# Written order of every engine's instructions for the whole program, instead of for its first part only: delta rule and gated feed-forward on one core

## The chip, the cores and the metric

The kernel runs on one core of a Trainium2 chip. The time is the device time of one execution in microseconds: before the change 883.39 us, the median of three runs (882.07 to 884.29). The profiled execution has a span of 881.3 us.

A core has a matrix engine (PE, TensorE), VectorE (DVE in the profile), ScalarE (ACT), GpSimd (POOL) and SyncE (SP), which here only issues DMAs. Each of them works through its own stream of instructions in the order of the stream, and waits for the others through semaphores. The question of this case is only the order of the streams.

## The reference

Two blocks follow one another. The first is the delta rule over 768 tokens, for 4 batches of 8 heads with 48 elements each:

```python
k_n = k / (np.linalg.norm(k, axis=-1, keepdims=True) + 1e-06)
for t in range(S):
    y[:, :, t] = einsum('bhd,bhde->bhe', q[:, :, t], state)
    v_old = einsum('bhde,bhd->bhe', state, kt)
    state = state + bt * einsum('bhd,bhe->bhde', kt, vt - v_old)
```

The second is a gated feed-forward on the result, seen as 3072 tokens of 384 elements, with 1536 inner columns:

```python
xn = x / sqrt(mean(x * x) + 1e-06) * rms_g
g = xn @ w_gate
out = (g * sigmoid(g) * (xn @ w_val)) @ w_out
```

All is in float32. The weights arrive as 64-bit numbers, and the kernel itself turns them into float32.

## The kernel before

The 768 tokens of a sequence are cut into 6 chunks of 128. A chunk of one batch is a unit, so a chunk has 4 units and the program 24. Inside a chunk the recurrence is solved in blocks: the scores of keys against keys give a triangular matrix for each head, whose 32-wide diagonal blocks are inverted on VectorE for all batches and heads at once. This is `invert`: 31 pairs of a product `tmp` and a sum into `ttb`. The inverse goes to DRAM as `td`, and a second matrix as `nd`; from there `tt` and `ne` are read back in the layout that PE needs.

```python
def invert(c, dt):
    nc.gpsimd.memset(ttb, 0.0)
    ...
    for i in range(W - 1):                       # W = 32
        nc.vector.scalar_tensor_tensor(out=tmp, in0=gblk[...], scalar=nbeta[...], in1=ttb[...], ...)
        nc.vector.tensor_tensor(out=to, in0=to, in1=tmp, op=ALU.add)     # to: part of ttb
        ...
        yield dt
    nc.sync.dma_start(out=td, in_=ttb)
    nc.vector.tensor_tensor(out=gblk, in0=ttb..., in1=nbeta..., op=ALU.mult)
    for b in range(B):
        for a in (1, 3, 0, 2):
            nc.sync.dma_start(out=tt[b][...], in_=td[...])
        if b == 0:
            nc.sync.dma_start(out=nd, in_=gblk)
        for a in (0, 2):
            nc.sync.dma_start(out=ne[...], in_=nd[...])
    yield dt
```

`gblk`, the scores that `invert` starts from, comes the same way through DRAM: `gather` sends the blocks `gd` on ScalarE's queue, unit by unit, and after the fourth unit `gblk` is read on SP's queue. Ahead of that stands `prepare`, for each unit: the norm of the keys (a square on ScalarE, a sum on VectorE, a power on GpSimd), transposes of queries and keys on PE (`p_t`), scores (`p_g`), their copies on ScalarE and masked copies on VectorE.

`recur` is the chain of a chunk. Its steps `corner` (small products `p_v` and `p_w`, which read `tt` and `ne`), `inner` (`p_z`, `p_x`) and `outer` (`p_k`, `p_y`, `p_s`) are run for four units, shifted against one another:

```python
for s in range(-3, B + 2):
    inner(s, s - 1, s + 1)
    yield dt
    outer(s + 1, s - 1)
    yield dt
    corner(s + 3, s + 2)
    ... # scale and transpose the results of units s - 1 and s - 2 (p_xt)
    yield dt
```

`ffn` is the feed-forward of two units, 256 tokens. It has 12 steps f; the output product `leave` of a step comes one step later, so that the silu on ScalarE and the product `h_f` on VectorE have time:

```python
def ffn(m, f0, f1):
    ...
    for f in range(f0, f1):
        p_gv = psum.tile([128, 2, TOK], FP32, name="p_gv", tag="gv", bufs=2)
        for i, w_sb in enumerate((wg_sb, wv_sb)):
            for t in range(KT):                                   # KT = 3
                nc.tensor.matmul(p_gv[:, i], w_sb[:, t, ...], xt[:, t], ...)
            yield 1
        nc.scalar.activation(out=sil, in_=p_gv[:, 0], func=ACTF.Silu)
        nc.vector.tensor_tensor(out=h_f, in0=sil, in1=p_gv[:, 1], op=ALU.mult)
        if last is not None:
            leave(f - 1, last)                                    # two matmuls, 128x384: p_o
            yield 1
        last = h_f
    yield 0.9
    leave(f1 - 1, last)
    ...
```

At the end of an `ffn` two outputs thus stand next to each other. The first two feed-forwards (m = 0 and 1) are run in halves of 6 steps, because the weights are still being converted on VectorE (`weights`: five instructions of 128x768 for each block of weights, written with their own times).

All these parts are Python generators. A plan gives each a start time, and the number that a generator yields is the time to its next piece. The plan is run in order of time, in its own units, about one for three gate matmuls; what it writes is the program:

```python
def at(time, gen):
    plan.append((time, len(plan), gen))

def run_plan(until=math.inf):
    heap = plan
    heapq.heapify(heap)
    while heap and heap[0][0] < until:
        t, i, gen = heapq.heappop(heap)
        dt = next(gen, None)
        if dt is not None:
            heapq.heappush(heap, (t + dt, i, gen))

TF = 68
CYC = 3 * FT * B // 2                                             # 72
at(0, setup())
...
at(49, recur(0, 1.5, 3))
for i, m in enumerate((0, 1, 0, 1)):
    at(TF + CYC // 4 * i, ffn(m, half_f * (i // 2), half_f * (i // 2 + 1)))
...
for c in range(1, NCH):
    t0 = TF - 16 + CYC * c
    first = TF + 2 if c == 1 else t0 - 60
    for b in range(B):
        at(first + 4.5 * b, prepare(B * c + b))
    at(first + 27, invert(c, 0.68))
    at(*((t0 - 4, recur(c, 0.9)) if c == 1 else (t0 - 9, recur(c, 1.2))))
    for g in range(B // 2):
        at(t0 + 16 + CYC // 2 * g, ffn(B // 2 * c + g, 0, FT))
with tc.manual_schedule():
    run_plan(TF + CYC // 2)
run_plan()
```

What is written inside `tc.manual_schedule()` stays, on each engine, in the order in which it is written. What is written outside of it is put in order by the framework's scheduler, which goes by its own estimates of when each instruction can run; it may also set such instructions between those of the first group.

Of the kernel before, what the change touches and what calls it, by code (L numbers as in the profile page):

```python
# [27 lines left out]
def kernel(  # L28
# [739 lines left out]
    plan = []  # L768
# [1 line left out]
    def at(time, gen):  # L770
        plan.append((time, len(plan), gen))

    def run_plan(until=math.inf):
        heap = plan
        heapq.heapify(heap)
        while heap and heap[0][0] < until:
            t, i, gen = heapq.heappop(heap)
            dt = next(gen, None)
            if dt is not None:
                heapq.heappush(heap, (t + dt, i, gen))  # L780


    TF = 68
    CYC = 3 * FT * B // 2
# [25 lines left out]
        for g in range(B // 2):  # L810
            at(t0 + 16 + CYC // 2 * g, ffn(B // 2 * c + g, 0, FT))
    with tc.manual_schedule():
        run_plan(TF + CYC // 2)
    run_plan()


# [28 lines left out]
```

## Time and profile before

| | |
|---|---|
| time | 883.39 us (882.07 to 884.29) |
| span of the profiled execution | 881.3 us |
| PE busy | 828.5 us, 94% |
| weight loads of PE (PEld) busy | 646.7 us, 73% |
| VectorE busy | 404.7 us, 46% |
| ScalarE busy | 259.0 us, 29% |
| GpSimd busy | 97.7 us, 11% |
| gate and value products (p_gv) in the chain that ended last | 36% of the span |
| output products (p_o) in that chain | 18% |
| tmp and ttb of the inversion in that chain | 4% and 3% |
| mean granted clock of PE | 0.96 |

The page divides the span into 40 slices of 22 us and gives for each the busy tenths of every engine and the clock that PE was granted, in tenths of full speed. In the timeline a line has start and length in us, engine, source line, operation, output and inputs, shapes and the number of instructions merged; in brackets stands how long the engine was idle ahead of it and what released it. PE's matmuls are pipelined, so that the lengths of neighbours overlap; what the matmuls take is read from start to start.

### The profile page before, as it was taken

What the parts mean: (1) busy time and instruction counts of PE and PEld (TensorE: products, weight loads), DVE (VectorE), ACT (ScalarE), POOL (GpSimd) and SP (SyncE); (2) the same over time, 40 slices, a digit from 0 to 9 for tenths busy, and PEclk for the clock granted to TensorE, in tenths of its full rate; (3) what the DMA queues carried; (4) which work ended last, traced back from release to release, by engine and by line L of the source; (5) the groups of instructions that cost most, each with busy time, mean ns of one, the idle gap of its engine ahead of it and who ended that gap; (6) DMA issues with size and microseconds to landing.
All of it is one profiled execution on the core that took longest, in us unless ns stands there. A gap on an engine that the chain in (4) does not pass through costs nothing.

```text
span 881.3 us, 19880 instructions
## 1 busy us (share of the span) xinstructions
PE 828.5 (94%) x8434; PEld 646.7 (73%) x8434; DVE 404.7 (46%) x997; ACT 259.0 (29%) x691; POOL 97.7 (11%) x136
## 2 busy tenths in 40 slices
PE   6487798989999999999999999999999999999998
PEld 5376665767877777787777787777787777777776
DVE  3786677886243393243392243492332491221110
ACT  4622345511424312324311324212334212221101
POOL 3000144200041000131000131000130000010000
PEclk8576799999999999999999999999999999999999
DMA  7615536502222103122103122103121103000000
GB/s 182 169 45 133 145 98 157 151 2 75 57 56 49 46 18 86 31 63 39 47 18 85 38 56 41 46 18 85 39 55 23 36 23 80 2 20 1 18 1 18
DMA packets 150935, 51.81 MB, mean 59 GB/s; under 512 B 142368, under 2 KB 145440, under 8 KB 150848
## 3 DMA queue, kind: packets, MB, share of 16 engines
q1 hardware_dynamic: 124736, 47.40, 21.2%
q10 hardware_dynamic: 26112, 3.15, 2.2%
q8 instruction: 66, 1.08, 0.5%
q14 instruction: 21, 0.17, 0.1%
HBM read 36.37 MB, written 14.16 MB: 57 GB/s over the span
## 4 chain that ended last, share of the span: by engine, by line
PE 72%; DVE 9%; DMA 2%; ACT 2%; issue 1%; POOL 1%; ACTq 0%; SPq 0%
PE p_gv L732 36%; PE p_o L719 18%; DVE tmp L428 4%; DVE ttb L437 3%; PE p_g L329 3%; PE p_y L531 2%; PE p_t L313 2%; PE p_k L569 2%; PE p_z L587 2%; PE p_y L569 2%; PE p_x L605 1%; PE p_v L497 1%; PE p_z L596 1%; DMA gblk<-gd 1%; PE p_s L550 1%; DVE h_f L743 1%
## 5 line engine op out<-in xcount | busy, mean ns | idle before, releaser
L719 PE MATMUL p_o<-wo_sb,h_f 128*128 128x384 f32 x576 | 215.8, 497 | 11.1 <-DVE h_f L743 11.1
L732 PE MATMUL p_gv<-xt,wg_sb 128*128 128x256 f32 x864 | 217.3, 388 | 0.0
L732 PE MATMUL p_gv<-xt,wv_sb 128*128 128x256 f32 x864 | 213.6, 383 | 0.0
L732 PEld LDWEIGHTS p_gv<-xt,wg_sb 128*128 128x128 f32 x864 | 161.6, 193 | 39.4 <-issue 0.6
L732 PEld LDWEIGHTS p_gv<-xt,wv_sb 128*128 128x128 f32 x864 | 161.5, 190 | 24.4 <-issue 2.5
L743 DVE TENSOR_TENSOR h_f<-sil,p_gv 128x256 f32<-128x256 f32 x144 | 60.1, 418 | 241.3 <-ACT sil L741 241.1
L741 ACT ACTIVATE sil<-p_gv 128x256 f32<-128x256 f32 x144 | 55.1, 383 | 342.8 <-PE p_gv L732 314.7
L719 PEld LDWEIGHTS p_o<-wo_sb,h_f 128*128 128x128 f32 x576 | 104.0, 190 | 62.7 <-DVE h_f L743 16.7
L428 DVE SCALAR_TENSOR_TENSOR tmp<-gblk,nbeta,ttb 128x31 f32<-128x31 f32 (+15 forms) x186 | 74.7, 402 | 11.5 <-DMA gblk<-gd 4.7
L437 DVE TENSOR_TENSOR ttb<-ttb,tmp 128x31 f32<-128x31 f32 (+15 forms) x186 | 63.6, 342 | 6.6 <-PE p_g L329 0.5
L343 DVE TENSOR_TENSOR gp<-p_g,mask 64x128 f32<-64x128 f32 (+1 forms) x160 | 37.9, 277 | 40.0 <-ACT gp L339 35.6
L329 PE MATMUL p_g<-kqt 64*64 64x192 f32 (+2 forms) x896 | 46.3, 331 | 9.5 <-ACT gp L339 4.8
L329 PEld LDWEIGHTS p_g<-kqt 64*64 64x64 f32 x896 | 34.1, 147 | 20.1 <-ACT gp L339 6.5
L293 POOL TENSOR_TENSOR knrm<-ksum,half 128x8 f32<-128x8 f32 x24 | 42.4, 1765 | 2.0
L688 POOL TENSOR_SCALAR ms<-ms 128x1 f32<-128x1 f32 x24 | 5.9, 247 | 328.0 <-ACT y L680 327.8
L318 ACT COPY kqt<-p_t 128x512 f32<-128x512 f32 x48 | 28.0, 584 | 40.2 <-PE p_t L313 37.9
L420 POOL MEMSET ttb<- 128x1024 f32 x6 | 6.1, 1021 | 261.5 <-DMA td<-ttb 246.0
L587 PEld LDWEIGHTS p_z<-v_raw,tt 64*64 64x64 f32 x768 | 26.1, 142 | 8.8 <-issue 6.7
L512 ACT COPY vs<-p_v 32x256 f32<-32x256 f32 x48 | 17.4, 362 | 49.4 <-PE p_w L504 28.1
L338 ACT COPY gp<-p_g 128x128 f32<-128x128 f32 x96 | 25.5, 265 | 20.3 <-PE p_g L329 18.4
L605 PE MATMUL p_x<-tt,gp 64*64 64x64 f32 x384 | 29.0, 229 | 1.8 <-ACT tt L514 1.8
L531 PE MATMUL p_y<-u,gp 128*64 128x48 f32 x768 | 26.6, 222 | 3.4 <-DVE u L612 3.2
(87 smaller groups left out, 798.6 us busy)
## 6 DMA issues: line engine op xcount, KB each, us to landing
kpad<-in_k_dram SPq DMA_DIRECT2D x24, 192.0 KB, 2.6
raw<-in_moe_w_gate_dram SPq DMA_DIRECT2D x6, 768.0 KB, 5.0
qpad<-in_q_dram SPq DMA_DIRECT2D x24, 192.0 KB, 2.8
raw<-in_moe_w_val_dram SPq DMA_DIRECT2D x6, 768.0 KB, 4.7
v_raw<-in_v_dram SPq DMA_DIRECT2D x24, 192.0 KB, 3.0
raw<-in_moe_w_out_dram SPq DMA_DIRECT2D x6, 768.0 KB, 4.3
out_dram<-o_sb SPq DMA_DIRECT2D x24, 192.0 KB, 1.9
gd<-gp ACTq DMA_DIRECT2D x96, 32.0 KB, 1.7
```

The costliest lines, as they stand in the source:

```text
L293: nc.gpsimd.tensor_tensor(out=knrm, in0=ksum, in1=half, op=ALU.pow)
L329: nc.tensor.matmul(to, pair[d, K1 if i else K0], pair[d, places], skip_group_check=True)
L343: nc.vector.tensor_tensor(out=to[p, :, place], in0=p_g[p, :, place], in1=mask[p, i, None].to_broadcast([p.stop, 2, HC]), op=ALU.mult,)
L428: nc.vector.scalar_tensor_tensor(out=tmp, in0=gblk[:, i, None, i + 1 :].to_broadcast(shape), scalar=nbeta[:, c, i : i + 1], in1=ttb[:, 0 : ...
L437: nc.vector.tensor_tensor(out=to, in0=to, in1=tmp, op=ALU.add)
L531: nc.tensor.matmul(p_y[p, h], gp[b_y][:, h, HC * place : HC * (place + 1)], u[:, h], start=(c == 0 and h == 0), stop=True, skip_group_chec ...
L587: nc.tensor.matmul(p_zs[b_z][p, h], tt[b_z][p, h], r[p, h], start=(h == 0), stop=(p is lo), skip_group_check=True,)
L605: nc.tensor.matmul(p_x[lo, h], gp[b_x][hi, h, HC * K0 : HC * (K0 + 1)], tt[b_x][hi, h], skip_group_check=True,)
L719: nc.tensor.matmul(p_o[i], h_f[:, i * C : (i + 1) * C], wo_sb[:, f], start=(f == f0), stop=(f == f1 - 1),)
L732: nc.tensor.matmul(p_gv[:, i], w_sb[:, t, f * 128 : (f + 1) * 128], xt[:, t], start=(t == 0), stop=(t == KT - 1),)
L741: nc.scalar.activation(out=sil, in_=p_gv[:, 0], func=ACTF.Silu)
L743: nc.vector.tensor_tensor(out=h_f, in0=sil, in1=p_gv[:, 1], op=ALU.mult)
```

## The change

The plan is no longer run in two parts. The whole of it is written inside `tc.manual_schedule()`, so that each engine follows the plan's order to the end, where before the scheduler ordered everything with a plan time of 104 (TF + CYC/2) or later. It is meant to give the author of the plan, not the scheduler's estimates, the last word on what each engine does next. No instruction is added, removed or altered.

```diff
-    def run_plan(until=math.inf):
-        heap = plan
+    def run_plan():
+        heap = list(plan)
         heapq.heapify(heap)
-        while heap and heap[0][0] < until:
+        while heap:
             t, i, gen = heapq.heappop(heap)
             dt = next(gen, None)
             if dt is not None:
@@
     with tc.manual_schedule():
-        run_plan(TF + CYC // 2)
-    run_plan()
+        run_plan()
```

## The prediction

> **What bounds the kernel now.** I read the page first, then the granted clock and busy times by stage, then who PE waits for, then PE's and VectorE's instructions in order of time around each wait. The page's busy slices:
>
> ```profile
> PE   6487798989999999999999999999999999999998
> DVE  3786677886243393243392243492332491221110
> PEclk8576799999999999999999999999999999999999
> ```
>
> A slice is 22 us. From the tenth on PE is full; before that it has holes and a low clock. A busy PE row proves little, since ends of matmuls are modelled, so I timed the work. Each matmul leaves two records. In the timeline one feed-forward step f (six gate and value matmuls, two output matmuls) takes 2.59 + 1.29 = 3.88 us wherever nothing else lies between, and that is the same at 198 us and at 870 us. There are 144 such steps: 144 x 3.88 = 559 us. A chunk of the recurrence repeats every 130.5 us (its double output product is at 451.3, 581.8 and 712.3); 24 steps are 93 us of it and the remaining 37 are PE's recurrence matmuls. So PE bounds the kernel, and only PE's own idle time can be won or lost. Who PE waited for after 200 us:
>
> ```profile
> PE p_o L719 <- DVE h_f L743: 4.1, 5, 1.6
> ```
>
> The columns are total, times, longest. Only 4 us are idle in the last 680, so the change can win almost nothing there. The rest of the idle time lies before 200 us. Where the regions of old and new order meet, PE shows:
>
> ```profile
> 179.55 1.56 PE L719 MATMUL p_o<-wo_sb,h_f 128*128 128x384 f32 x4 [1.08 <-DVE h_f L743]
> 180.94 1.46 PE L732 MATMUL p_gv<-xt,wg_sb 128*128 128x256 f32 x6
> 182.24 1.46 PE L732 MATMUL p_gv<-xt,wv_sb 128*128 128x256 f32 x6
> 186.41 1.60 PE L719 MATMUL p_o<-wo_sb,h_f 128*128 128x384 f32 x4 [2.72 <-DVE h_f L743]
> 187.81 2.76 PE L732 MATMUL p_gv<-xt,wg_sb 128*128 128x256 f32 x6
> 190.37 1.88 PE L732 MATMUL p_gv<-xt,wv_sb 128*128 128x256 f32 x6
> ```
>
> Counting steps from 1, these are output 11, gates 13, output 12, gates 14. Output 12 waits for VectorE's product h_f of step 12, which stands behind weight conversion and the inversion of chunk 1:
>
> ```profile
> 185.08 0.95 DVE L274 SCALAR_TENSOR_TENSOR wo_sb<-raw,wo_sb 128x768 f32<-128x768 uint32 x1
> 185.95 0.41 DVE L743 TENSOR_TENSOR h_f<-sil,p_gv 128x256 f32<-128x256 f32 x1
> ```
>
> VectorE runs there without a gap, so it, not PE, sets the pace until 187. And gates 14, 4.3 us instead of 2.6, are slow: the granted clock is 0.50 from 188 to 190 and 0.70 to 192, a penalty of 1.7 us after the wait.
>
> **What the Trainium skill says.** "TensorE: Matmul & The Clock Gate", section "Part 1: The HAM clock gate", has the clock halved after an idle window of about 3.4 us, with a free-running window. The trace agrees in kind: 2.7 us idle at 184 and 3.1 at 147 are each followed by a clock near 0.5; 1.6 us idle at 450 is not. The same page's "Architectural detail" section says that ScalarE's and VectorE's queues are strict FIFO. The trace agrees: every wait above is a product queued behind other work. "Perfetto Trace Analysis", section "Identifying the Most-Contended Engine", calls matmul busy time a bad measure of headroom; here 98% busy and the timed steps happen to agree.
>
> **The change part by part.** No instruction is added or removed. What was in written order only for plan times below 104 is now so throughout. Placing the streams of both builds side by side:
>
> (1) PE. Identical up to output 11, and again from about step 25 on, save single outputs and the choice of buffers. Between, output 12 moves ahead of gates 13, and the first recurrence product of chunk 1 (p_v) comes after output 17 instead of after gates 20. The chain itself is more spread between steps.
>
> Working for chunk 1. VectorE's stream is the same to the product of step 12, so output 12 still starts at 186.4, but gates 13 now lie after it instead of inside the wait: PE idles from 180.9 to 186.4, 5.5 us, and is 2.6 behind. From 187.8: gates 13 to 18 are 6 x 2.59 = 15.5, outputs 13 to 17 are 5 x 1.29 = 6.5, the slow clock 1.7 again; PE is at p_v at 211.5. Does the inverse arrive? Now td (the inverse, to DRAM) is issued at:
>
> ```profile
> 210.41 0.34 SPq L445 DMA_DIRECT2D td<-ttb  x1
> ```
>
> In the new order VectorE doesn't wait 1.33 us for a gate product at 192.7 and has one product fewer (0.33) ahead of it, and its later products come after their gates; hence about 209.2 (some 0.5 open). The new order sends the first tt blocks ahead of nd, as the first chunk does in both kernels; there p_v ran 5.3 us after td (62.5 to 67.8). So p_v starts at 214.5, with PE idle 3.0. At 218.4 the kernel before had done p_v, gates 19 and 20, outputs 18 and 19. The new one needs after 214.5: 0.6 for p_v and 2 x 3.88, and is there at 222.9: **4.5 us behind**, plus 0.9 for an even chance of another 1.7 us slow clock.
>
> What comes back: before, the rest of that chain is dense. From 218.4 to the last transpose of chunk 1 (269.4) are 51.0 us with six steps (23.3) and two key or query transposes (0.9): 26.8 for the chain. In the chunk starting at 471.0, whose steps alternate as the new order has them, the same stretch is 66.6 minus ten steps (38.8), minus transposes and scores (2.8), minus p_v (0.6): 24.4. The dense one runs v and w, z and x one after the other, where the spread one mixes them on different rows (0.69 for v and w together, 0.62 each alone). So **-2.5 us**. Chunk 1: 4.5 + 0.9 - 2.5 = +2.9.
>
> (2) VectorE in the inversions of chunks 2 to 5. PE's order is the same there, but the products h_f sit elsewhere between the 31 pairs of tmp and ttb. At the end of a feed-forward of 12 steps two outputs stand back to back, and the second waits for its h_f. Before, in the chunk at 581:
>
> ```profile
> 581.01 0.42 DVE L437 TENSOR_TENSOR ttb<-ttb,tmp 128x255 f32<-128x255 f32 x1
> 581.36 0.41 DVE L743 TENSOR_TENSOR h_f<-sil,p_gv 128x256 f32<-128x256 f32 x1
> ```
> ```profile
> 581.82 1.56 PE L719 MATMUL p_o<-wo_sb,h_f 128*128 128x384 f32 x4 [0.74 <-DVE h_f L743]
> ```
>
> 14.5 pairs and two products precede that h_f; in the new order 16 pairs and three do. Extra: 1.5 pairs x 0.95 + 0.33 = 1.75. But the new inversion may start ahead of a product it now stands behind: gblk is issued at 564.74, lands 3.3 later (page, median), and the sends on ScalarE come about 0.35 later behind one silu, so 568.4 instead of 568.95: -0.55. Net **+1.2 us each, four times: +4.8**. In the chunk at 451 the wait is 1.6 already and 2.8 might drop the clock; I leave this to the range.
>
> (3) ScalarE, GpSimd and SP. Key norms of the next chunk come later, silu stands behind copies and ksq. I followed each silu and h_f through one chunk with the durations before (silu 0.38, eight gp copies 2.2, four sends 1.8, ksq 0.5, the power on GpSimd 1.67): the latest are 0.5 to 2 us ahead of their outputs, so nothing on PE's path. The closest is the output at 520.0, with 0.5 us left. Nothing in (3) is counted.
>
> Sum: 883.4 + 2.9 + 4.8 = **891**.
>
> **Rivals.** First: the written order is the better tuned one, and the time falls. For it: its chain in chunk 1 is denser in mixed products, and hoisted norms no longer hold up VectorE (it waited 1.8 us for one at 157). Against it: VectorE then waits for gblk at 176.9 anyway, and PE's idle time after 200 us is 4 us in all. At best the first wait costs nothing and the h_f shift vanishes: 881. Second: a strict order turns small delays into stalls in each chunk, for instance tt blocks of the second batch behind nd and ne, or silu behind ksq, at 0.5 us margins. With two such stalls of 1 us per chunk and slow clocks behind each wait: 900 to 905. Third: all of it hides, since PE's order hardly differs: 884 to 886; against that stand outputs 12 and p_v, which are pinned by VectorE.
>
> **Range and chances.** Chunk 1 may be +1 to +6, by tt's landing and the clock; chunks 2 to 5 +2 to +9. Together 886 to 897 holds eight in ten. 2% is 17.7 us: 866 can't be reached with 4 us of idle time to win; 901 needs the second rival in every chunk.
>
> **What would show it.** PE idle about 5.5 us ahead of the output at 186.4; p_v idle 2 to 4 us near 212, released by tt; about 1 to 2 us more wait for h_f at each double output (near 321, 453, 584, 714); other PE waits absent. Wrong would be: td well below 209, gblk landing earlier, so that h_f comes in time, or waits on ScalarE in the recurrence.

## The result and the profile after

The changed kernel takes **889.15 us** (median; 887.27 to 890.23) against 883.07 us (882.07 to 884.29) for the kernel before, measured side by side: a ratio of 1.0066, with a 95% interval of 1.0044 to 1.0088. It is 6 us slower, 0.7%. Its profiled execution has a span of 886.8 us. Its page has these busy slices:

```profile
PE   5487798968999999999999999999999999999998
DVE  3786577995234293233393234392233491221010
PEclk9577699988999999999999999999999999999999
```

From the eleventh slice on PE is as full as before. Apart from small differences in the first five slices, where both kernels have the same order on PE, the ninth and tenth differ, some 177 to 222 us: PE has 6 and 8 tenths where it had 8 and 9, and the clock 8 and 8 where it had 9 and 9. Who PE waited for from 170 us to the end (line, releaser; total, times, longest):

```profile
PE p_o L719 <- DVE h_f L743: 11.4, 6, 5.3
PE p_v L497 <- DMA tt<-td: 2.7, 4, 1.7
```

The second group didn't exist before. PE's timeline of the changed kernel in the two places where the prediction put the loss, output 12 and the first recurrence product of chunk 1:

```profile
178.78 1.56 PE L719 MATMUL p_o<-wo_sb,h_f 128*128 128x384 f32 x4 [1.37 <-DVE h_f L743]
185.65 2.93 PE L719 MATMUL p_o<-wo_sb,h_f 128*128 128x384 f32 x4 [5.31 <-DVE h_f L743]
...
209.59 1.45 PE L719 MATMUL p_o<-wo_sb,h_f 128*128 128x384 f32 x4
212.78 0.22 PE L497 MATMUL p_v<-tt,gp 32*32 32x32 f32 x2 [1.74 <-DMA tt<-td]
213.51 1.05 PE L497 MATMUL p_v<-tt,gp 32*32 32x32 f32 x30 [0.51 <-DMA tt<-td]
214.49 2.93 PE L719 MATMUL p_o<-wo_sb,h_f 128*128 128x384 f32 x4
217.22 2.77 PE L732 MATMUL p_gv<-xt,wg_sb 128*128 128x256 f32 x6
219.78 1.65 PE L732 MATMUL p_gv<-xt,wv_sb 128*128 128x256 f32 x6
221.26 1.46 PE L732 MATMUL p_gv<-xt,wg_sb 128*128 128x256 f32 x6
```

The wait of output 12 is 5.31 us instead of 2.72, and p_v waits 1.74 and 0.51 us for tt, where PE didn't wait before. What follows p_v is slow, too: from start to start output 18 takes 2.73 us instead of 1.29, and the two halves of gates 19 take 2.56 and 1.48 instead of 1.29 each. That is 1.44 + 1.27 + 0.19 = 2.9 us lost. The stretch from 214 us by granted clock (columns: stretch, length, busy time and instructions of PE, PEld, DVE, ACT and POOL, clock, DMA share, GB/s):

```profile
214.00:220.00 6.00, 6.00 (x31) 4.19 (x28) 1.11 (x2) 0.73 (x2) 0.00 (x0) 0.50 0.43 115
```

At the double outputs of the later chunks the changed kernel waits 1.33, 1.17, 1.09 and 1.09 us for h_f, where the kernel before waited 0.75, 1.61, 0.74 and 0.74. The wait that corresponds to the one shown of the kernel before at 581.82, in PE's timeline and then in VectorE's:

```profile
586.98 1.56 PE L719 MATMUL p_o<-wo_sb,h_f 128*128 128x384 f32 x4 [1.09 <-DVE h_f L743]
```
```profile
586.51 0.41 DVE L743 TENSOR_TENSOR h_f<-sil,p_gv 128x256 f32<-128x256 f32 x1
```

And one thing that the prediction had named only in a rival. In chunk 2 SP's queue issues nothing for 4.5 us after `nd`:

```profile
341.15 0.39 SPq L461 DMA_DIRECT2D nd<-gblk  x1
345.67 0.80 SPq L463 DMA_DIRECT2D ne<-nd  x2
346.51 1.92 SPq L456 DMA_DIRECT2D tt<-td  x4
```

`ne` can't be read before `nd` has landed, and the tt blocks of the second batch stand behind it. p_v of that batch runs about 1.0 us after PE reached it, in two waits (348.54 and 349.16).

**Where the 6 us came from.** The order up to output 11 is the same in both kernels, and its start differs by chance (179.55 before, 178.78 after), so I count from there. From output 11 to the first double output: 140.36 us before, 145.17 after, that is +4.81, of which 0.58 is that output's own longer wait. Then from double output to double output +0.77, +0.35 and +0.35, and from the last to the end 168.96 against 168.95. So in these two profiles chunk 1 costs 4.2 us and all later ones 2.1, together 6.3.

### The profile page after: what moved, and what is told of

The parts are those of the page before. It is cut to its first block, busy times and chain, and to the rows that moved or that the text cites. A ratio compares the mean times of both kernels' runs of the same rounds, so it can differ in the third digit from the quotient of the medians.

```text
span 886.8 us, 19834 instructions
## 1 busy us (share of the span) xinstructions
PE 827.0 (93%) x8434; PEld 644.8 (73%) x8434; DVE 404.6 (46%) x997; ACT 256.0 (29%) x691; POOL 96.4 (11%) x136
## 4 chain that ended last, share of the span: by engine, by line
PE 67%; DVE 11%; DMA 5%; ACT 2%; issue 1%; SPq 0%; ACTq 0%; POOL 0%; DVEq 0%
PE p_gv L732 33%; PE p_o L719 16%; DVE tmp L428 5%; DVE ttb L437 4%; PE p_g L329 3%; PE p_y L531 2%; DMA gblk<-gd 2%; PE p_t L313 2%; PE p_k L569 2%; PE p_z L587 2%; PE p_y L569 2%; DMA gd<-gp 1%; PE p_x L605 1%; PE p_v L497 1%; DVE h_f L743 1%
## 5 line engine op out<-in xcount | busy, mean ns | idle before, releaser
L719 PE MATMUL p_o<-wo_sb,h_f 128*128 128x384 f32 x576 | 217.0, 500 | 14.5 <-DVE h_f L743 14.5
L680 ACT ACTIVATE y<-p_y 128x384 f32<-128x384 f32 x24 | 11.8, 491 | 92.6 <-PE p_y L531 92.6
```

The source lines that it names most:

```text
L719: nc.tensor.matmul(p_o[i], h_f[:, i * C : (i + 1) * C], wo_sb[:, f], start=(f == f0), stop=(f == f1 - 1),)
```

## The experiments

The theory was that of the prediction: VectorE pins output 12 and p_v in chunk 1, and h_f is late at the double outputs of the later chunks. The times below were measured beside the kernel before (883.2 us or within 0.4 of it each time). A single execution of the kernel before came out anywhere from 878.5 to 886.4 us, and the intervals show that a ratio is good to 1 to 2 us. The last column of the table removes part of that scatter from the profiled execution: it is the span less the start of output 11. In ten of these executions, the kernel before among them, whose PE order is the same up to output 11, that start lay anywhere from 178.0 to 181.9 us. The column still stands for one execution each, and not always a usual one: the profiled execution was the fastest of its kernel with the scheduler from 104 to 176 only (884.85 against a median of 888.21), with the last outputs later (885.67 against 889.35) and with the chain later and nd first (881.59 against 884.12), and the slowest with nd first (890.58 against 888.66).

| kernel | median, us | ratio to before (95%) | output 11 to the end, us |
|---|---|---|---|
| before | 883.07 | 1 | 701.8 |
| changed | 889.15 | 1.0066 (1.0044 to 1.0088) | 708.0 |
| written order up to plan time 176 | 885.65 | 1.0041 (1.0022 to 1.0061) | 703.6 |
| scheduler from 104 to 176 only | 888.21 | 1.0063 (1.0040 to 1.0085) | 704.8 |
| output 12 later | 888.40 | 1.0071 (1.0049 to 1.0093) | 706.5 |
| chain of chunk 1 later | 884.84 | 1.0020 (1.0007 to 1.0033) | 702.6 |
| last outputs later | 889.35 | 1.0066 (1.0045 to 1.0087) | 708.7 |
| nd first | 888.66 | 1.0052 (1.0036 to 1.0069) | 706.6 |
| useless products in both waits | 887.09 | 1.0040 (1.0026 to 1.0054) | 705.0 |
| chain later, last outputs later, nd first | 881.04 | 0.9975 (0.9959 to 0.9991) | 700.9 |
| chain later, last outputs later | 884.26 | 1.0016 (1.0001 to 1.0032) | 703.5 |
| chain later, nd first | 884.12 | 1.0013 (1.0003 to 1.0024) | 701.2 |
| chain later, useless products at output 12 | 882.52 | 0.9996 (0.9984 to 1.0009) | 700.1 |
| the three and useless products | 884.54 | 1.0025 (1.0012 to 1.0037) | 703.9 |

### Half of the change at a time

The plan is cut at 176 (TF + CYC*3/2), which separates chunk 1 from the rest, save that the preparation and the inversion of chunk 2, planned from 136 and 163 on, begin before the cut. The two edits are shown against the kernel before.

```diff
 # written order up to plan time 176
     with tc.manual_schedule():
-        run_plan(TF + CYC // 2)
+        run_plan(TF + CYC * 3 // 2)
     run_plan()
```

> The written order holds up to plan time 176 (TF + CYC*3/2), the scheduler's from there on, so that chunk 1 has the changed kernel's order and chunks 2 to 5 that of the kernel before. Theory (most of the loss is in chunk 1: output 12 pinned ahead of gates 13, p_v ahead of its data, slow clock after both): about 887.5, 4 to 5 us above the kernel before. Rival (most of the loss is the shifted h_f and the late tt in chunks 2 to 5, as my prediction's sum had it with 4.8 of 7.7): about 885 to 886.

```diff
 # scheduler from 104 to 176 only
     with tc.manual_schedule():
         run_plan(TF + CYC // 2)
-    run_plan()
+    run_plan(TF + CYC * 3 // 2)
+    with tc.manual_schedule():
+        run_plan()
```

> The complement: the scheduler orders what has plan times from 104 to 176 (chunk 1), everything else is in written order. PE's stream is then that of the kernel before throughout, and VectorE's, ScalarE's and SP's are the changed kernel's from chunk 2 on. Theory: about 885, 2 us above the kernel before (0.35 to 0.6 more wait at each of three double outputs, 1 us for late tt in chunk 2). Rival: 887 to 888. The two costs should add up to the 6 us of the whole change within 1 us.

The first half costs 3.6 us by its ratio (0.0041 x 883), the second 5.6; the profiles, counted from output 11, give 1.8 and 3.0. My expectations of the sizes fell: both medians lie where the rivals had them (885.65 and 888.21), and the two costs don't add up to 6 within 1 us. Each half shows the waits that were expected of it: the first has 5.31 us at output 12 and 1.84 and 0.41 at p_v, and the usual 0.73 at the later double outputs; the second has the old 2.72 at output 12 and, from chunk 3 on, 1.25, 1.16 and 1.22 at the double outputs. So both parts of the prediction exist. Their sizes aren't settled by this pair: the medians add up to 9.2, the profiles to 4.8, and the whole is 6. The profile of the second half is that of its fastest execution. In the first half the scheduler moved an output between the gates in chunk 2, so that its first double output doesn't wait at all, which may make it cheaper than chunk 1 of the whole change; this isn't shown.

### Is VectorE what pins chunk 1?

If output 12 waits because it stands too early on PE, a later place wins 2.6 us. If VectorE sets the pace anyway, p_v waits longer instead.

```diff
 # output 12 later: after gates 13, as before
-        p_o = [psum.tile([128, DM], FP32, name="p_o", tag="out", bufs=2) for i in range(2)]
+        p_o = []                                  # the two tiles are taken at the first leave
 ...
-        yield 0.9
+        yield 2.9 if (m, f0) == (1, 0) else 0.9
```

The output tiles `p_o` are taken later here, and likewise in each edit below that moves the last outputs.

> The changed kernel, with only the last output of the second feed-forward half two plan units later, behind gates 13 as in the kernel before. Theory (VectorE, not PE, sets when p_v can start, so what PE saves at output 12 it waits at p_v): the wait at output 12 falls from 5.3 to about 2.7 us, the one at p_v grows from about 2.4 to about 5, and the time stays at 888 to 889. Rival (the two waits are independent costs): 2.6 us or more are won, 886.

Nothing is won: 1.0071 against 1.0066. Output 11 and PE's waits behind it in its timeline:

```profile
180.32 1.56 PE L721 MATMUL p_o<-wo_sb,h_f 128*128 128x384 f32 x4 [1.28 <-DVE h_f L745]
187.19 1.56 PE L721 MATMUL p_o<-wo_sb,h_f 128*128 128x384 f32 x4 [2.72 <-DVE h_f L745]
193.73 1.56 PE L721 MATMUL p_o<-wo_sb,h_f 128*128 128x384 f32 x4 [2.39 <-DVE h_f L745]
214.10 0.28 PE L497 MATMUL p_v<-tt,gp 32*32 32x32 f32 x2 [3.29 <-DMA tt<-td]
```

The wait is down to 2.72 as in the kernel before, but 2.39 us reappear at the next output and p_v waits 3.29 + 0.29 instead of 1.74 + 0.51. Counted from the start of output 11, p_v's first products start at 33.78 us here and at 34.00 in the changed kernel (214.10 - 180.32 and 212.78 - 178.78), although PE's waits ahead of them differ; with all last outputs later and with useless products, both below, it is 33.82 and 33.64. So PE doesn't set this time: the inverse must be finished on VectorE and have been through DRAM.

The counter-test lets PE do feed-forward work while it would wait for tt: the chain of chunk 1 starts three plan units later.

```diff
 # chain of chunk 1 later
-        at(*((t0 - 4, recur(c, 0.9)) if c == 1 else (t0 - 9, recur(c, 1.2))))
+        at(*((t0 - 1, recur(c, 0.8)) if c == 1 else (t0 - 9, recur(c, 1.2))))
```

> The changed kernel, with the chain of chunk 1 started 3 plan units later and run at 0.8 instead of 0.9 per piece; p_v then stands behind gates 20. Theory: the wait for tt (2.4 us) and the slow clock after it (2.9 us) are gone, a denser chain gives 1 to 2 us back: 885 to 886. Rival (p_v's place costs nothing net, because the denser chain loses as much as the wait): 889.

884.84, so 4.1 us of the 6 come back by the ratios, 5.4 by the profiles (708.0 and 702.6). No wait for tt is left in chunk 1 (the one below is in chunk 2), and 198 to 220 us run at full clock. From its list of PE's waits from 170 us on, and the stretch by stage:

```profile
...
PE p_v L497 <- DMA tt<-td: 1.1, 1, 1.1
```
```profile
198.00:220.00 22.00, 22.00 (x154) 16.64 (x154) 13.91 (x35) 3.02 (x8) 0.00 (x0) 1.00 0.22 65
```

The wait for tt (2.25) and the slow clock behind it (2.9) are 5.15 together, close to what the profiles say was won. The edit also runs the chain at 0.8 instead of 0.9 a piece; what that is worth alone wasn't measured, but the two waits leave only 0.3 us for it. This is the largest part of the change's cost, and it lies in one place.

### The double outputs and SP's queue

Here the later chunks are concerned. One edit moves each last output but the program's very last two plan units later, the other sends nd right after td.

```diff
 # last outputs later
-        yield 0.9
+        yield 0.9 if (m, f1) == (NU // 2 - 1, FT) else 2.9
```

> The changed kernel, with the last output of every feed-forward but the very last two plan units later, so that it stands behind the first gates of the next one and no two outputs are adjacent. Theory: the waits for h_f at the four double outputs of chunks 2 to 5 (1.3, 1.2, 1.1, 1.1 us in the changed kernel's trace) go, 4.7 us; output 12 gains nothing, because VectorE sets when p_v can start; 884 to 885. Rival (VectorE paces these places too, so that the wait only moves to a later output or to p_v): 888 to 889.

```diff
 # nd first
+        if c > 0:
+            nc.sync.dma_start(out=nd, in_=gblk)
         for b in range(B):
             ...
-            if b == 0:
+            if b == 0 and c == 0:
                 nc.sync.dma_start(out=nd, in_=gblk)
```

> The changed kernel, with nd sent ahead of the tt blocks in chunks 1 to 5, as the scheduler had it in the kernel before, so that the second batch of tt doesn't stand behind a late nd on SP's queue. Theory (what the traces of single executions show least of, but the medians of the last runs ask for: late tt costs chunks 2 to 5 some 2 to 3 us in a usual execution): 886 to 887, with no wait of p_v for tt beyond chunk 1. Rival (only the 1 us seen in chunk 2 counts): 888.

The first wins nothing (889.35), and my expectation of 884 to 885 fell. PE's waits from 170 us on show that they moved:

```profile
PE p_o L721 <- DVE h_f L745: 7.3, 7, 2.7
PE p_v L497 <- DMA tt<-td: 4.8, 2, 3.3
PE p_gv L734 <- DVE xt L703: 2.6, 4, 0.7
```

PE waits 4.1 us less for h_f, but 2.1 more for tt and 2.6 at the first gates of the next feed-forward, whose input xt VectorE now finishes too late. That is as the rival had it. The second edit wins at most 1.2 us, less than its interval can tell; in its profile no wait for tt is left but chunk 1's, so what there was to win was the 1 us of chunk 2, as the rival had it.

### What the slow clock costs

Useless 128x128 products, which add to no result, are set into both waits of chunk 1: 22 ahead of output 12 and 10 ahead of p_v.

```diff
 # useless products in both waits
+    def fill(n):
+        p_f = ps_delta([128, DM], "p_fill2")
+        for i in range(n):
+            nc.tensor.matmul(p_f[:, 0:128], ident, ident, ...)
 ...
+        if c == 1:
+            fill(10)                              # at the start of recur
+    at(TF + CYC // 2 - 0.15, fill_at(22))
```

> The changed kernel with 22 useless products of 128x128 ahead of output 12 and 10 ahead of chunk 1's first p_v, in PE's two long waits; they add to no result. Theory (4.9 us of the loss are the halved clock after these waits): the granted clock stays at 1.0 from 176 to 220, p_v is reached about 2 us earlier and waits that much longer (VectorE sets its start), and only the 2.9 us after p_v are won: 886. Rival (the slow clock lies in time that PE would wait anyway): 889. Should the products run longer than the wait, up to 1 us is lost.

PE's timeline:

```profile
180.24 1.56 PE L730 MATMUL p_o<-wo_sb,h_f 128*128 128x384 f32 x4 [1.43 <-DVE h_f L754]
181.63 5.08 PE L718 MATMUL p_fill<-ident 128*128 128x128 f32 x44
187.11 1.56 PE L730 MATMUL p_o<-wo_sb,h_f 128*128 128x384 f32 x4 [0.40 <-DVE h_f L754]
...
210.56 2.39 PE L718 MATMUL p_fill<-ident 128*128 128x128 f32 x20
213.88 0.22 PE L497 MATMUL p_v<-tt,gp 32*32 32x32 f32 x2 [0.92 <-DMA tt<-td]
214.67 0.69 PE L497 MATMUL p_v<-tt,gp 32*32 32x32 f32 x30 [0.57 <-DMA tt<-td]
215.28 2.77 PE L730 MATMUL p_o<-wo_sb,h_f 128*128 128x384 f32 x4
217.85 1.98 PE L743 MATMUL p_gv<-xt,wg_sb 128*128 128x256 f32 x6
219.66 1.46 PE L743 MATMUL p_gv<-xt,wv_sb 128*128 128x256 f32 x6
```

2.3 us are won by the ratios, 3.0 by the profiles, between the two expectations. The first filling keeps the clock up: output 12 runs at 1.56 and not 2.93, and PE is through with output 17 about 1.8 us earlier, counted from output 11 (at 30.32 us instead of 32.10). But p_v starts only 0.3 us earlier: the rest goes into the second filling and the waits for tt. So the slow clock behind output 12 cost hardly any time in the whole. Behind p_v the clock falls again, but for a shorter time: from start to start output 18 takes 2.57 us and the first half of gates 19 1.81, instead of 2.73 and 2.56. With the faster rest of p_v that is 1.5 us won up to gates 20. A further 1.1 us of the profile's gain lies in chunk 2, where no wait for tt is left because nd landed early in this execution; whether the useless products have a part in that isn't shown.

### Putting them together

> The changed kernel with the chain of chunk 1 later (3 units, 0.8 a piece), every last output later, and nd first. If the three gains add up (4.1 measured, 4.5 and 2 expected): about 878 to 880, below the kernel before. Rival (the gains share the same waits): 882 to 884.

The three edits together take 881.04 us, 0.9975 of the kernel before, between the two expectations. By the medians that is more than the edits won one by one (8.0 us against 4.1, 0 and 1.2). Two runs with one part left out and two with useless products were to tell why.

> The later chain of chunk 1 together with the last outputs two plan units later, without the earlier nd. Measured so far: the later chain alone 884.8, the later outputs alone 889.4, the two with nd ahead of tt 881.0. Theory: later outputs won nothing by themselves because what they gave at output 12 was lost again in the wait for tt in chunk 1; with that wait gone they give about 2.6 us (output 12's wait 5.3 to 2.7), so 882. Rival: it was the earlier nd that made the three good together, and this one is at 884 to 885 like the later chain alone.

> The later chain of chunk 1 together with nd sent right after td from the second chunk on, outputs left in place. Theory (the later outputs are worth about 2.6 us once the chain is late): here 883.5 to 885, since only the wait of about 1 us for tt in chunk 2 goes. Rival (the earlier nd makes the three good): 881 to 882.

> The later chain of chunk 1 together with 22 useless 128 x 128 products ahead of output 12, which add to no result; they keep PE busy while it waits there for h_f. Theory: the slow clock after output 12's wait costs PE about 1.7 us, so 883 against 884.8 for the later chain alone, with a granted clock near 1.0 from 186 to 192. Rival: the 2.3 us won with useless products earlier came from chunk 1's second filling, so here there is no gain: 884.5 to 885.5.

> The three edits (later chain, later last outputs, nd ahead of tt from the second chunk on), together with 12 useless 128 x 128 products ahead of output 12, which add to no result and take about as long as its wait of 2.7 us. If the slow clock after that wait is what remains of the change's cost in the second half of the first chain, PE's gates after output 12 run at 2.6 us instead of 4.3, and the time falls from 881.0 to about 879.3. Rival: the useless products end late or the clock falls elsewhere (after the 0.7 us wait at the next output), and nothing is won: 881.

(1) With either the later outputs or the earlier nd left out the time stays at 884.1 to 884.3, so by the medians neither edit alone explains the gain; it takes both. The profiles show the part of the earlier nd, in PE's waits in chunk 2, 300 to 450 us. Without it:

```profile
PE p_v L497 <- DMA tt<-td: 1.1, 1, 1.1
...
```

With all three this line is absent, and the others are the same to 0.1 us. In chunk 1 it is likewise a wait of 0.83 us for tt that goes. Together that is 1.95 of the 2.65 us between the two profiles (703.5 and 700.9). The part of the later outputs isn't shown: without them the profile has 701.2 us, only 0.3 more than with all three, in an execution that was the fastest of its kernel (881.59). So what makes the 3 us between these two medians stays open.

(2) Filling output 12's wait beside the later chain gives 882.52 against 884.84, 2.1 us by the ratios, as the theory had it, and the clock stays at 1.00 from 186 to 192 us. But the profiles place most of the gain elsewhere. PE is 1.9 us ahead at output 13, then output 18 waits 0.99 us for h_f, where it didn't wait before, and at gates 19 only 0.5 us are left. The larger piece, 1.4 us, is won in chunk 2, where the wait for tt is gone. SP's queue there:

```profile
337.15 0.39 SPq L461 DMA_DIRECT2D nd<-gblk  x1
340.03 0.80 SPq L463 DMA_DIRECT2D ne<-nd  x2
```

From nd to the first read of it are 2.88 us here, where the later chain alone has 4.99. This is the same in the kernel with useless products in both waits (2.87, against 4.52 in the changed kernel). So the median of this pair doesn't measure the slow clock.

With all three edits, useless products give 884.54 against 881.04, the opposite of what I expected. PE's timeline of all three, and then of all three with useless products:

```profile
185.02 1.76 PE L723 MATMUL p_o<-wo_sb,h_f 128*128 128x384 f32 x4 [2.72 <-DVE h_f L747]
186.57 2.77 PE L736 MATMUL p_gv<-xt,wg_sb 128*128 128x256 f32 x6
...
191.56 1.56 PE L723 MATMUL p_o<-wo_sb,h_f 128*128 128x384 f32 x4 [0.70 <-DVE h_f L747]
```
```profile
182.59 2.84 PE L718 MATMUL p_fill<-ident 128*128 128x128 f32 x24
185.48 1.56 PE L732 MATMUL p_o<-wo_sb,h_f 128*128 128x384 f32 x4
...
192.02 1.56 PE L732 MATMUL p_o<-wo_sb,h_f 128*128 128x384 f32 x4 [2.40 <-DVE h_f L756]
```

The gates are fast now, but the next output waits 2.40 for h_f instead of 0.70 and starts 6.54 us after output 12 in both. Here the slow clock was hidden behind VectorE, so nothing could be won. What was lost besides, by the profiles 3.5 us, lies in chunks 4 and 5, where the double output waits 1.75 us instead of 0.54 and 0.70: in that execution the blocks gd landed late. In chunk 4 they were sent at the same moment to within 0.04 us, yet SP issued gblk only at 562.79 instead of 560.95. The gd blocks' own times to landing between 556 and 566 us, of the three edits and then with useless products, were:

```profile
DMA to landing us min/median/max: 1.5/1.7/3.2
```
```profile
DMA to landing us min/median/max: 1.5/3.1/3.8
```

The profiled execution is a usual one of this run (884.58, median 884.54). Whether the useless products have a part in the late landing, or it is the chip, stays open: the two runs lie on different chips, and the three edits alone were measured once, with 9 executions. So their lead over the kernel before, 0.25%, is about what such a delay takes away, and it isn't shown to hold everywhere.

## Why the prediction was right, and which of its terms were off

**Right: the time, and the mechanism in chunk 1.** The prediction added 2.9 us for chunk 1 and 4.8 for the later ones, 891.0 in all; 889.15 was measured. Each of the waits it named is in the profile, with the releaser it named, and no wait of PE on ScalarE or GpSimd turned up. That p_v's place on PE, ahead of its data, makes the loss of chunk 1 is confirmed by the two shifts there: moving output 12 won nothing, moving the chain won most of the loss. Two of its signs failed: the waits for h_f at the double outputs were to grow by 1 to 2 us each, and other waits of PE were to be absent. The waits at the double outputs grew by 0.58 at most, and p_v waited for tt in chunk 2. The split between the two parts is the other way round in the profiles: 4.2 and 2.1. By the medians of the halves (3.6 and 5.6) it would be nearer to the predicted one. I trust the profiles' sizes more for single waits, since these recur in every variant that keeps the outputs in place and has the new order in these chunks (0.98 to 1.26 in chunks 3 to 5), but what the second half's median holds beyond its waits stays open.

**Output 12** (predicted: idle from 180.9 to 186.4, PE 2.6 behind): 5.31 idle instead of 2.72, which is 2.6. Right. The slow clock after it, put at 1.7 again, took 1.95.

**p_v** (td at 209.2, tt 5.3 later, p_v at 214.5, idle 3.0): td was issued at 208.41, which is 209.2 with the 0.77 us by which this execution was early. SP's queue:

```profile
208.41 0.34 SPq L445 DMA_DIRECT2D td<-ttb  x1
```

p_v's first products came 4.4 us later and the others 5.1, so PE was idle 2.25. The term was too large by 0.75.

**The slow clock after p_v** (predicted: even chance of 1.7, so 0.9): it came and cost 2.9. This is the largest miss in chunk 1. The size was taken from the slow spell after output 12, where PE gets half the clock for some 3.4 us (0.95, 0.50 and 0.70 in the three stretches of 2 us from 186); here it was 6. The Trainium skill, "TensorE: Matmul & The Clock Gate", section "Part 1: The HAM clock gate", speaks of an idle window of about 3.4 us; here 1.74 and 0.51 us, with p_v's first products between, were enough.

**The rest of the chain, more spread in the new order** (predicted: 2.5 us come back): put together, 4.5 - 0.75 + 2.9 = 6.65 us should have been missing ahead of it. At the last transpose of chunk 1 (268.96 before, 272.68 after), counted from output 11, 4.5 are missing. So some 2.2 came back. This is by subtraction, not measured by itself.

**h_f in chunks 2 to 5** (predicted +1.2 each): +0.58, -0.44, +0.35 and +0.35. In the chunk whose working was shown both halves of the term were off. The work ahead of the product is more by 1.18 us (13.59 against 12.41 from the start of the inversion to h_f), not 1.75: I had counted 14.5 pairs for the kernel before, and its timeline shows 15, so the difference is one pair, not 1.5. And the inversion starts 0.84 us earlier against PE's place, not 0.55, because it no longer stands behind a product but starts as gblk lands. 1.18 - 0.84 = 0.34. In chunk 3 the old wait was 1.61 already, so that the new order even gains there.

**SP's queue** (named as a rival, counted 0): about 1.0 us in chunk 2, in this execution.

So the sum came this close partly by luck: by the profiles chunk 1 was put 1.3 us too low and the later chunks 2.7 too high, and the two errors half cancel.

## What to carry to other kernels

A wait moves with its cause. When an engine other than the full one sets a time (here VectorE with the inverse), moving the full engine's instructions only moves the idle time, unless they are brought to where the late result is needed: put independent work ahead of the first instruction that waits for the late result, and leave the rest. After such a wait look at the granted clock of the next 6 us, for the slow spell can cost more than the wait (2.9 us against 2.25 here), but count it only where PE and not another engine sets what comes next. And edits that shift waits must be tried together: here, by the medians, the later outputs and the earlier nd were worth little until both were in.

## What the runs showed of the hardware

- **A wait's length alone doesn't decide whether the clock falls.** After 2.72 us ahead of output 12 it fell with all three edits (the first half of gates took 2.77 instead of 1.46); after the same 2.72 us in the kernel with only the later output 12 it didn't (1.46), nor after its next wait of 2.39. After p_v's waits of 0.92 and 0.57 us, right behind useless products, it did. What else decides isn't shown here. The spells that were timed from start to start took 1.7 to 2.9 us.
- **The same order doesn't start alike.** The start of output 11 scatters over 3.9 us between ten executions with the same PE order up to there. Differences below that mean something only when counted from a common point.
- **A DMA of the same size, issued at the same place in the order, can take half as long again or more.** From nd of chunk 2 to the first read of it were 4.52 us in the changed kernel and 4.99 with the later chain, but 2.87 and 2.88 in the two kernels that have useless products and keep nd in its place. Why is not shown.
